# One two-bank PSUM tile for both pairs of heads, and one operation for both, in the attention's products

## The chip, the cores and the metric

The kernel runs on one core of one Trainium2 chip. The metric is the device time of the whole kernel in microseconds (us), as the median of several runs.

## The reference

Two layers follow each other. The first is attention by the delta rule, with 4 batches, 8 heads, 768 steps and a head width of 48:

```python
k_n = k / (norm(k) + 1e-6)
for t in range(S):
    y[:, :, t] = einsum('bhd,bhde->bhe', q[:, :, t], state)
    v_old = einsum('bhde,bhd->bhe', state, kt)
    state = state + bt * einsum('bhd,bhe->bhde', kt, vt - v_old)
```

The second is a rational feed-forward layer on the 3072 rows of 384 that the attention gives (`d_ff` is 2048):

```python
h = x @ w_in
P = a[0] + a[1]*h + a[2]*h**2 + a[3]*h**3
Q = 1 + |b[0]|*|h| + |b[1]|*h**2
out = (P / (Q + 1e-6)) @ w_out
```

## The kernel before

The 768 steps are cut into 12 chunks of 64. A chunk of all four batches is worked at once: 128 partitions are two batches by 64 steps, and the other factor of two of the batches is the **pair** `p` (`PAIRS`, two of them), each with 8 heads. So a product of the attention has 16 small results of 48 or 64 columns, 8 for each pair. `mm3` (L401) makes them: for each pair 24 matmuls (8 heads, 3 passes of float16 halves), first pair 0, then pair 1. `bank` (L418) gives each pair a PSUM tile of its own, one bank of 512 float32 columns. ACT and DVE then take the result out with an operation for each pair, so twice for each product, each on 8*48 = 384 or 8*64 = 512 columns.

A chunk goes through these products: `pg` (keys by keys, taken out by ACT at L528), `pm` (keys by queries, DVE, L667), `pe` (blocks off the diagonal, `split16` at L614), `pk` (the state's part of the residual, DVE, L687), `pu` (the solve), `pd` (the state's update, DVE, L719) and `py` (the outputs, ACT, L734). The solve is a chain: `solve_start` writes `pu`, and three times `solve_step` (L698) reads `pu`, makes two float16 halves `z` of it (ACT writes the upper half at L229, DVE the rest at L233), and adds the product of `z` to `pu`. `solved` reads `pu` once more (ACT L227, DVE L231), `state_next` multiplies that and adds it to the state `S16`, and the next chunk's `state_split`, `residual` and solve start from `S16`. So the chunks' solves form one chain through the kernel. `tokens` (L739) scales the outputs of a chunk and transposes them into `xT`, with `px` in PSUM and `split16` at L762.

The feed-forward layer takes a chunk's `xT` in 8 **units** `n` (96 in all): `hidden` multiplies (`ph`, L818), `numerator` and `quotient` compute the fraction (L835 to L865, each operation on 512 columns; `mu`, `mw`, `mr` and `mg` are their tiles), and `accumulate` multiplies into `po` (L880). Unit 8c is the first of chunk c and can't start before `xT` of chunk c and the scalars `msc` (L802) are there.

PSUM has 8 banks: `ps_f` two tiles of a bank (`pg`, `pm`, `pe`, small totals, and `px` from chunk 3 on), `ps_c` two (`pk`, `pu`, `pd`, `py`, and `px` of the first chunks), `ps_h` two, `ps_o` two. The order of the instructions on each engine comes from a scheduler that places them by priorities and by its own estimates (L1054); the attention's steps of chunks c+1 to c+4 are issued among the units of chunk c (`attention`, L977), and those of the solve with a raised priority. Each engine then runs its instructions strictly in the order so found.

Of the kernel before, what the change touches and what calls it, by code (L numbers as in the profile page):

```python
# [36 lines left out]
def kernel(  # L37
# [29 lines left out]
    TG = NPAIR * P  # L67
# [13 lines left out]
    sb = ctx.enter_context(tc.tile_pool(name="sb", bufs=2))  # L81
    dpool = ctx.enter_context(tc.tile_pool(name="dpool", bufs=2, space=DRAM))
    dfix = ctx.enter_context(tc.tile_pool(name="dfix", bufs=1, space=DRAM))
    ps_f = ctx.enter_context(tc.tile_pool(name="ps_f", bufs=2, space=PSUM))
    ps_c = ctx.enter_context(tc.tile_pool(name="ps_c", bufs=2, space=PSUM))
    ps_h = ctx.enter_context(tc.tile_pool(name="ps_h", bufs=2, space=PSUM))
    ps_o = ctx.enter_context(tc.tile_pool(name="ps_o", bufs=1, space=PSUM))

# [148 lines left out]
    def parts(t):  # L237
        return t[:, 0], t[:, 1]
# [5 lines left out]
        nc.gpsimd.tensor_scalar(x, x, scale, 0.0, op0=ALU.mult, op1=ALU.add)  # L244

    def total(src, n, nm, pool=ps_f, tag="a"):
        pf = pool.tile([P, n], F32, tag=tag, name="pf" + nm)
        nc.tensor.matmul(pf, ones, src, start=True, stop=True)
        return pf

# [166 lines left out]

    def bank(pool, nm, w):  # L418

        made = []  # L420
        for p in PAIRS:
            t = pool.tile([P, 512], F32, tag="a", name=f"{nm}_{p}")
            made.append(t[:, : H * w].rearrange("p (h w) -> p h w", w=w))
        return made

    def of(t, p):

        return t[:, p * H : (p + 1) * H]

    def of_parts(t, p):  # L430
        return of(t[:, 0], p), of(t[:, 1], p)
# [29 lines left out]
    def transposed(x, src, nm, soon):  # L461


        split16(
            [x[:, i, :, :, :D].rearrange("p h b d -> p b h d") for i in range(2)],
            src.rearrange("p (b h) d -> p b h d", b=2),
            eng=nc.gpsimd,
            hi=nc.gpsimd,
        )
        xd = dpool.tile([2, NH, P, HG, 2, DP], F16, tag="xd" + nm[0], name=f"xd{nm}", bufs=4 if nm[0] == "k" else 2)  # L470
        nc.sync.dma_start(
            out=xd.rearrange("i n r a b d -> r (i n) (a b d)"),
            in_=x.rearrange("r i (n a) b d -> r (i n) (a b d)", n=NH),
        )
        t = sb.tile([P, 2, NH, NPAIR, C, HG], F16, tag="tt", name="t" + nm)
        if soon:
            for i in range(2):
                pt = ps_f.tile([P, H, P], F16, tag="a", name=f"pt{nm}_{i}")
                for h in range(H):
                    nc.tensor.transpose(pt[:, h], x[:, i, h].rearrange("p b d -> p (b d)"), ident16)  # L480
                for n in range(NH):
                    nc.scalar.copy(
                        t[:, i, n].rearrange("x p t a -> x a (p t)"), pt[:, n * HG : (n + 1) * HG]
                    )
            return t, xd
        nc.sync.dma_start(
            out=t.rearrange("x i n p t a -> x (i n p t a)"),
            in_=xd.rearrange("i n r a b d -> (i n r a) (b d)"),
            transpose=True,
        )  # L490
        return t, xd
# [29 lines left out]
    def key_products(c):  # L521
        d = info[c]
        gd = d["gd"] = dpool.tile([P, BS], F32, tag="gd", name=f"gd_{c}")
        pg = bank(ps_f, f"pg_{c}", C)
        mm3(pg, d["kbd"], d.pop("tk"))
        g = sb.tile([P, HP, C], F32, tag="g", name=f"g_{c}", bufs=1)
        for p in PAIRS:
            nc.scalar.mul(of(g, p), pg[p], -1.0)  # L528
        for b in range(2):
            nc.sync.dma_start(out=as_rows(gd, b), in_=g[b * C : (b + 1) * C])  # L530
        gl = sb.tile([P, HP, C - 16, 2], F16, tag="gl", name=f"gl_{c}", bufs=1)
        split16([gl[..., i] for i in range(2)], g[:, :, : C - 16], eng=nc.gpsimd, hi=nc.gpsimd)
        d["gl"] = gl
# [71 lines left out]
    def off_blocks(c):  # L605

        d = info[c]
        gbd, wc = d.pop("gbd"), d.pop("wc")
        pe = bank(ps_f, f"pe_{c}", C - 16)
        mm3(pe, gbd, wc[:, :, 16:])  # L610
        d["wbd"] = to_diagonal("w", wc)
        et = sb.tile([P, 2, HP, C - 16], F16, tag="u0", name=f"et_{c}", bufs=1)
        for p in PAIRS:
            split16(of_parts(et, p), pe[p], 1.0 / 256.0)  # L614
        ebd = d["ebd"] = diag["e"][0]
        for b in range(2):
# [43 lines left out]
    def query_products(c):  # L660

        d = info[c]
        pm = bank(ps_f, f"pm_{c}", C)
        mm3(pm, d["kbd"], d["tq"])
        m32 = sb.tile([P, HP, C], F32, tag="g", name=f"m32_{c}", bufs=1)
        for p in PAIRS:
            nc.vector.tensor_mul(of(m32, p), pm[p], mask.unsqueeze(1).broadcast_to([P, H, C]))  # L667
        mm = d["mm"] = sb.tile([P, 2, NG, C, HG], F16, tag="mm", name=f"mm_{c}", bufs=1)
        split16([alternating(mm[:, i]) for i in range(2)], grouped(m32), eng=nc.gpsimd)

# [9 lines left out]
    def residual(c):  # L680
        d = info[c]
        rf = d.pop("vs")
        if c > 0:
            pk = bank(ps_c, f"pk_{c}", D)
            mm3(pk, d["kbd"], d["sh"])
            for p in PAIRS:
                nc.vector.scalar_tensor_tensor(  # L687
                    out=of(rf, p), in0=of(rf, p), scalar=d["sv"], in1=pk[p], op0=ALU.mult, op1=ALU.subtract
                )
        d["rr"] = sb.tile([P, 2, HP, D], F16, tag="z", name=f"rr_{c}", bufs=2)  # L690
        split16(parts(d["rr"]), rf, eng=nc.gpsimd)

# [5 lines left out]
    def solve_step(c, it):  # L698

        d = info[c]  # L700
        z = sb.tile([P, 2, HP, D], F16, tag="z", name=f"z_{c}_{it}", bufs=2)
        for p in PAIRS:
            split16(of_parts(z, p), d["pu"][p], zmask[:, it : it + 1])
        mm3(d["pu"], d["ebd"], z, start=False)

    def solved(c):
        d = info[c]
        d["z"] = sb.tile([P, 2, HP, D], F16, tag="z", name=f"z_{c}", bufs=2)
        pu = d.pop("pu")
        for p in PAIRS:  # L710
            split16(of_parts(d["z"], p), pu[p])

    def state_next(c):
        d = info[c]
        pd = bank(ps_c, f"pd_{c}", D)
        mm3(pd, d["knbd"], d["z"])
        if c > 0:
            for p in PAIRS:
                nc.vector.scalar_tensor_tensor(  # L719
                    out=of(S16, p), in0=pd[p], scalar=d["isv"], in1=of(S16, p), op0=ALU.mult, op1=ALU.add  # L720
                )
        else:
            for p in PAIRS:
                nc.scalar.activation(of(S16, p), pd[p], AF.Copy, scale=d["isv"])

    def outputs(c):
        d = info.pop(c)
        py = bank(ps_c, f"py_{c}", D)
        if c > 0:
            mm3(py, d["qbd"], d["sh"], stop=False)  # L730
        mm3(py, d["mbd"], d["z"], start=c == 0)
        y = ys[c] = sb.tile([P, NPAIR, DM], F32, tag="ob", name=f"y_{c}", bufs=1)
        for p in PAIRS:
# [5 lines left out]
    def tokens(c):  # L739
# [318 lines left out]
```

## Time and profile before

| what | value |
|---|---|
| runs shown | 890.34, 892.65, 892.75 us; median 892.65 us |
| profiled execution, its own time | 895.27 us |
| its span | 893.4 us |
| busy: DVE | 800.4 us (90%) |
| busy: PE | 675.1 us (76%) |
| busy: ACT | 579.7 us (65%) |
| busy: POOL | 468.4 us (52%) |

The engines run side by side, so the busy times overlap. The first of the 96 units starts its DVE work at 151.26 us; before that the weights are converted and chunk 0 goes through the attention. The view by line gives for each group of instructions the busy time, the mean duration of one, and the idle time ahead of them. The view by time gives the starts, from which one sees how long an instruction really keeps its engine: the next one often starts before the last has ended.

### The profile page before, as it was taken

The page shows a single profiled execution, that of the slowest core. Times are in us where ns is not written, and L with a number is a line of the kernel's source. Part 1 is how long each engine was busy: PE and PEld are TensorE (multiplying, and loading weights), DVE is VectorE, ACT ScalarE, POOL GpSimd, SP SyncE. Part 2 cuts the span into 40 slices and gives each one's busy share as a digit, 9 for nine tenths or more (in the row PEclk, how much of TensorE's full clock was granted, in tenths as well). Part 3 has the DMA queues.
Part 4 walks back from the last instruction along what each step waited for, and adds up shares of the span by engine and source line. Part 5 has one row for each costly group of instructions (what it writes and reads, how often), then busy time and mean ns, then how long its engine had stood idle before and what let it go on. Part 6 is the DMA issues. An engine that isn't in the chain of part 4 may idle for free.

```text
span 893.4 us, 23555 instructions
## 1 busy us (share of the span) xinstructions
PE 675.1 (76%) x9264; PEld 540.8 (61%) x9264; DVE 800.4 (90%) x1666; ACT 579.7 (65%) x1122; POOL 468.4 (52%) x430
## 2 busy tenths in 40 slices
PE   0231454878597697988859989969989799899885
PEld 0221444766485585766648757758767677777563
DVE  5999898898888779879998799999999999898996
ACT  4776766647665483857657657667669476878574
POOL 6664754626446245466654574754745645353622
PEclk9999976978998897999988999989999899999998
DMA  8969978578858867879377469487485553200000
GB/s 234 231 165 196 207 173 158 95 144 143 160 115 147 172 136 137 140 144 186 57 164 123 95 132 167 79 181 139 84 191 94 112 108 58 67 1 19 1 19 18
DMA packets 420110, 111.49 MB, mean 125 GB/s; under 512 B 361376, under 2 KB 416672, under 8 KB 420000
## 3 DMA queue, kind: packets, MB, share of 16 engines
q1 hardware_dynamic: 417824, 108.83, 61.8%
q8 instruction: 72, 1.18, 0.6%
q10 hardware_dynamic: 2176, 1.17, 0.4%
q14 instruction: 38, 0.31, 0.1%
HBM read 40.47 MB, written 26.23 MB: 75 GB/s over the span
## 4 chain that ended last, share of the span: by engine, by line
DVE 33%; PE 22%; DMA 15%; SPq 11%; issue 8%; ACT 8%; POOL 3%; ACTq 0%; DVEq 0%; POOLq 0%
PE ph L818 7%; PE po L880 5%; SPq L441 4%; DVE mw L860 3%; DMA tq<-xdq 3%; PE pg L409 3%; DVE mu L838 2%; DVE mu L864 2%; DVE w_out L333 2%; DVE mw L840 2%; PE pm L409 2%; DVE mg L859 2%; PE pu L409 2%; DVE mu L842 2%; DMA wc<-img 2%
## 5 line engine op out<-in xcount | busy, mean ns | idle before, releaser
L818 PE MATMUL ph<-xT,w_in 128*128 128x256 f16 x1728 | 225.9, 286 | 30.3 <-DVE mu L842 29.5
L880 PE MATMUL po<-w_out,mg 128*128 128x384 f16 x1152 | 223.3, 340 | 28.8 <-POOL mg L865 27.0
L818 PEld LDWEIGHTS <-w_in 128*128 128x128 f16 x1728 | 174.1, 103 | 67.7 <-issue 18.1
L865 POOL TENSOR_TENSOR mg<-mu,mr 128x512 f16<-128x512 f32 x96 | 133.2, 1391 | 92.6 <-DVE mu L864 53.7
L880 PEld LDWEIGHTS <-mg 128*128 128x128 f16 x1152 | 110.5, 102 | 101.9 <-POOL mg L865 33.7
L835 ACT ACTIVATE mu<-ph,coef,msc 128x512 f32<-128x512 f32 x96 | 74.4, 775 | 60.7 <-DVE msc L802 25.0
L409 PEld LDWEIGHTS <-kbd 128*128 128x128 f16 x1680 | 93.6, 119 | 33.0 <-issue 28.2
L860 DVE SCALAR_TENSOR_TENSOR mw<-mw,msc,mg 128x512 f32<-128x512 f32 x96 | 88.0, 918 | 0.4
L838 DVE TENSOR_TENSOR mu<-ph,mu 128x512 f32<-128x512 f32 x96 | 65.5, 682 | 23.8 <-ACT mr L837 22.9
L841 ACT ACTIVATE mw<-mw 128x512 f32<-128x512 f32 x96 | 60.4, 630 | 35.5 <-DVE mw L840 35.1
L862 POOL TENSOR_TENSOR mu<-mu,mw 128x512 f32<-128x512 f32 x36 | 51.1, 1421 | 50.2 <-DVE mw L860 20.3
L840 DVE SCALAR_TENSOR_TENSOR mw<-mr,msc,ph 128x512 f32<-128x512 f32 x96 | 70.7, 737 | 0.0
L842 DVE SCALAR_TENSOR_TENSOR mu<-mu,msc,ph 128x512 f32<-128x512 f32 x96 | 70.5, 735 | 0.0
L853 ACT ACTIVATE mr<-mw,msc 128x512 f32<-128x512 f32 x96 | 69.2, 721 | 1.1
L409 PE MATMUL pu<-z,ebd 128*128 128x48 f16 x1728 | 56.1, 187 | 16.1 <-DVE z L233 12.3
L409 PEld LDWEIGHTS <-ebd 128*128 128x128 f16 x1728 | 54.5, 99 | 21.1 <-issue 19.0
L837 ACT ACTIVATE mr<-ph,msc 128x512 f32<-128x512 f32 x96 | 65.6, 684 | 0.0
L231 POOL TENSOR_TENSOR mm<-m,mm 128x1024 f16<-128x1024 f32 x12 | 31.6, 2632 | 64.0 <-ACT mm L227 56.2
L859 DVE SCALAR_TENSOR_TENSOR mg<-mu,msc,mr 128x512 f16<-128x512 f32 x60 | 60.7, 1012 | 2.5 <-ACT mr L854 2.5
L409 PEld LDWEIGHTS <-wbd 128*128 128x128 f16 x1152 | 37.1, 102 | 40.3 <-issue 26.2
L854 ACT ACTIVATE mr<-mr 128x512 f32<-128x512 f32 x96 | 60.4, 630 | 1.4
L846 POOL TENSOR_SCALAR mu<-mu,msc 128x512 f32<-128x512 f32 x36 | 28.9, 802 | 55.2 <-DVE mu L842 52.1
(201 smaller groups left out, 1435.7 us busy)
## 6 DMA issues: line engine op xcount, KB each, us to landing
wsi<-in_moe_w_in_dram SPq DMA_DIRECT2D x24, 256.0 KB, 4.9
xdk<-kn SPq DMA_DIRECT2D x12, 512.0 KB, 4.3
kbd<-tk SPq DMA_DIRECT2D x24, 256.0 KB, 4.3
gd<-g SPq DMA_DIRECT2D x24, 256.0 KB, 3.4
xdq<-kn SPq DMA_DIRECT2D x12, 512.0 KB, 3.5
wso<-in_moe_w_out_dram SPq DMA_DIRECT2D x32, 192.0 KB, 4.4
mbd<-mm SPq DMA_DIRECT2D x24, 256.0 KB, 4.9
wc<-img SPq DMA_DIRECT2D x24, 256.0 KB, 4.9
```

The costliest lines, as they stand in the source:

```text
L409: nc.tensor.matmul(dst[p][:, h], head(bd, lp, p * H + h), head(rt, rp, p * H + h), start=start and n == 0 and h == 0, stop=stop and n == l ...
L818: nc.tensor.matmul(ph[:, i], w_in[:, f2, wp, cc, i * P : (i + 1) * P], x[:, xp, cc], start=k == 0, stop=k == 3 * NCC - 1,)
L835: nc.scalar.activation(u, ph, AF.Identity, scale=A3, bias=a2)
L837: nc.scalar.activation(z, ph, AF.Abs, scale=B1)
L838: nc.vector.tensor_mul(u, ph, u)
L840: nc.vector.scalar_tensor_tensor(out=w, in0=z, scalar=B0, in1=ph, op0=ALU.add, op1=ALU.mult)
L842: nc.vector.scalar_tensor_tensor(out=u, in0=u, scalar=A1, in1=ph, op0=ALU.add, op1=ALU.mult)
L853: nc.scalar.activation(r, w, AF.Ln, bias=Q0)
L859: nc.vector.scalar_tensor_tensor(out=g[:, 0], in0=u, scalar=A0, in1=r, op0=ALU.add, op1=ALU.mult)
L860: nc.vector.scalar_tensor_tensor(out=w, in0=w, scalar=Q0, in1=g[:, 0], op0=ALU.add, op1=ALU.mult)
L865: nc.gpsimd.tensor_mul(g[:, 1], u, r)
L880: nc.tensor.matmul(po[p], g[:, gp, i, p * P : (p + 1) * P], w_out[:, f2, wp, i], start=f2 == lo and i == 0 and k == 0, stop=f2 == hi - 1 a ...
```

## The change

`bank` makes one tile of two banks, and gives a view for each pair and one of both. The pools `ps_f` and `ps_c` have one such tile each in the place of two of one bank. All matmuls stay, pair 0 first, each into a bank of its pair. Each operation that takes a product out covers both pairs: 768 columns in the place of twice 384, 1024 in the place of twice 512. In `tokens` the total, its copy to all partitions and the transposes share one tile, and the split covers both pairs. For `ps_f` every other user (`total`, the transposes of the first chunk) takes the whole tile of two banks.

```diff
+    ps_f = ctx.enter_context(tc.tile_pool(name="ps_f", bufs=1, space=PSUM))
+    ps_c = ctx.enter_context(tc.tile_pool(name="ps_c", bufs=1, space=PSUM))
...
     def total(src, n, nm, pool=ps_f, tag="a"):
-        pf = pool.tile([P, n], F32, tag=tag, name="pf" + nm)
+        pf = pool.tile([P, NPAIR * 512 if pool is ps_f else n], F32, tag=tag, name="pf" + nm)[:, :n]
...
     def bank(pool, nm, w):
-        made = []
-        for p in PAIRS:
-            t = pool.tile([P, 512], F32, tag="a", name=f"{nm}_{p}")
-            made.append(t[:, : H * w].rearrange("p (h w) -> p h w", w=w))
-        return made
+        t = pool.tile([P, NPAIR, 512], F32, tag="a", name=nm)[:, :, : H * w].rearrange("x p (h w) -> x p h w", w=w)
+        return t[:, 0], t[:, 1], t
+
+    def by_pair(t):
+        return t.rearrange("x (p h) d -> x p h d", p=NPAIR)
+
+    def parts_by_pair(t):
+        return by_pair(t[:, 0]), by_pair(t[:, 1])
...
         g = sb.tile([P, HP, C], F32, tag="g", name=f"g_{c}", bufs=1)
-        for p in PAIRS:
-            nc.scalar.mul(of(g, p), pg[p], -1.0)
+        nc.scalar.mul(by_pair(g), pg[2], -1.0)
...
-        for p in PAIRS:
-            split16(of_parts(et, p), pe[p], 1.0 / 256.0)
+        split16(parts_by_pair(et), pe[2], 1.0 / 256.0)
...
-        for p in PAIRS:
-            nc.vector.tensor_mul(of(m32, p), pm[p], mask.unsqueeze(1).broadcast_to([P, H, C]))
+        nc.vector.tensor_mul(
+            m32, pm[2].rearrange("x p h t -> x (p h) t"), mask.unsqueeze(1).broadcast_to([P, HP, C])
+        )
...
-            for p in PAIRS:
-                nc.vector.scalar_tensor_tensor(
-                    out=of(rf, p), in0=of(rf, p), scalar=d["sv"], in1=pk[p], op0=ALU.mult, op1=ALU.subtract
-                )
+            nc.vector.scalar_tensor_tensor(
+                out=by_pair(rf), in0=by_pair(rf), scalar=d["sv"], in1=pk[2], op0=ALU.mult, op1=ALU.subtract
+            )
...
         z = sb.tile([P, 2, HP, D], F16, tag="z", name=f"z_{c}_{it}", bufs=2)
-        for p in PAIRS:
-            split16(of_parts(z, p), d["pu"][p], zmask[:, it : it + 1])
+        split16(parts_by_pair(z), d["pu"][2], zmask[:, it : it + 1])
         mm3(d["pu"], d["ebd"], z, start=False)
...
-        for p in PAIRS:
-            split16(of_parts(d["z"], p), pu[p])
+        split16(parts_by_pair(d["z"]), pu[2])
...
-            for p in PAIRS:
-                nc.vector.scalar_tensor_tensor(
-                    out=of(S16, p), in0=pd[p], scalar=d["isv"], in1=of(S16, p), op0=ALU.mult, op1=ALU.add
-                )
+            nc.vector.scalar_tensor_tensor(
+                out=by_pair(S16), in0=pd[2], scalar=d["isv"], in1=by_pair(S16), op0=ALU.mult, op1=ALU.add
+            )
...
-        for p in PAIRS:
-            nc.scalar.activation(y[:, p].rearrange("p (h d) -> p h d", h=H), py[p], AF.Copy, scale=d["iy"])
+        nc.scalar.activation(y.rearrange("x p (h d) -> x p h d", h=H), py[2], AF.Copy, scale=d["iy"])
...
+        px = pool.tile([P, NPAIR * 512], F32, tag="a", name=f"px_{c}")
+        pf, pb = px[:1, NCC * TG : NCC * TG + P], px[:, NCC * TG + P : NCC * TG + P + 1]
...
+        px = px[:, : NCC * TG].rearrange("x (c t) -> x c t", t=TG)
         for p in PAIRS:
-            px = pool.tile([P, 512], F32, tag="a", name=f"px_{c}_{p}")[:, : NCC * P].rearrange("p (c t) -> p c t", t=P)
             for cc in range(NCC):
-                nc.tensor.transpose(px[:, cc], yt[:, p, cc * P : (cc + 1) * P], identf)
-            split16([x[:, i, :, p * P : (p + 1) * P] for i in range(2)], px, sx)
+                nc.tensor.transpose(px[:, cc, p * P : (p + 1) * P], yt[:, p, cc * P : (cc + 1) * P], identf)
+        split16(parts(x), px, sx)
```

The scheduler finds another order for the whole kernel. Two places on DVE show it. In the names the first number is the chunk or the unit, and `z_2_1` is `z` of the second solve step of chunk 2; the changed file's lines lie a few lower or higher.

DVE, from the second to the third solve step of chunk 2, before:

```order
L233 SCALAR_TENSOR_TENSOR z_2_1_3498<-pu_2_0_3231,zmask_85,z_2_1_3498 128x384
L233 SCALAR_TENSOR_TENSOR z_2_1_3498<-pu_2_1_3232,zmask_85,z_2_1_3498 128x384
L842 SCALAR_TENSOR_TENSOR mu9_3609<-mu9_3609,msc_1_3174,ph_9_3590 128x512
L859 SCALAR_TENSOR_TENSOR mg8_3620<-mu8_3482,msc_1_3174,mr8_3484 128x512
L576 TENSOR_REDUCE ab_3_2568<-pr_3_2567 128x64
L838 TENSOR_TENSOR mu10_3867<-ph_10_3848,mu10_3867 128x512
L840 SCALAR_TENSOR_TENSOR mw10_3872<-mr10_3869,msc_1_3174,ph_10_3848 128x512
L860 SCALAR_TENSOR_TENSOR mw8_3487<-mw8_3487,msc_1_3174,mg8_3620 128x512
L578 TENSOR_TENSOR pr_3_2567<-ab_3_2568,wt0_111 128x512
L233 SCALAR_TENSOR_TENSOR z_2_2_3625<-pu_2_0_3231,zmask_85,z_2_2_3625 128x384
L842 SCALAR_TENSOR_TENSOR mu10_3867<-mu10_3867,msc_1_3174,ph_10_3848 128x512
L233 SCALAR_TENSOR_TENSOR z_2_2_3625<-pu_2_1_3232,zmask_85,z_2_2_3625 128x384
```

The same place now:

```order
L234 SCALAR_TENSOR_TENSOR z_2_1_3426<-pu_2_3164,zmask_85,z_2_1_3426 128x768
L851 SCALAR_TENSOR_TENSOR mg10_4009<-mu10_3786,msc_1_3107,mr10_3788 128x512
L852 SCALAR_TENSOR_TENSOR mw10_3791<-mw10_3791,msc_1_3107,mg10_4009 128x512
L830 TENSOR_TENSOR mu12_4124<-ph_12_4105,mu12_4124 128x512
L832 SCALAR_TENSOR_TENSOR mw12_4129<-mr12_4126,msc_1_3107,ph_12_4105 128x512
L856 SCALAR_TENSOR_TENSOR mu10_3786<-mu10_3786,msc_1_3107,mw10_3791 128x512
L834 SCALAR_TENSOR_TENSOR mu12_4124<-mu12_4124,msc_1_3107,ph_12_4105 128x512
L502 TENSOR_REDUCE nrm_5_3732<-sq_5_3733 128x16
L851 SCALAR_TENSOR_TENSOR mg11_4135<-mu11_3998,msc_1_3107,mr11_4000 128x512
L234 SCALAR_TENSOR_TENSOR z_2_2_3551<-pu_2_3164,zmask_85,z_2_2_3551 128x768
```

Each step is one row of 768 columns that needs both pairs' matmuls and ACT's whole operation; between the two steps of pair 0 stood 7 rows of other work, and now 8 stand between the steps.

DVE ahead of unit 24, the first of chunk 3, before (the two rows of `S16` are the end of chunk 4's solve):

```order
L719 SCALAR_TENSOR_TENSOR S16_133<-pd_4_0_6185,sc_4_3560,S16_133 128x384
L719 SCALAR_TENSOR_TENSOR S16_133<-pd_4_1_6186,sc_4_3560,S16_133 128x384
L860 SCALAR_TENSOR_TENSOR mw21_5440<-mw21_5440,msc_2_4324,mg21_5523 128x512
L778 TENSOR_SCALAR kp_3_0_5452<-kp_3_0_5452,coef_99 128x1 x3
L838 TENSOR_TENSOR mu23_5618<-ph_23_5599,mu23_5618 128x512
L840 SCALAR_TENSOR_TENSOR mw23_5623<-mr23_5620,msc_2_4324,ph_23_5599 128x512
L233 SCALAR_TENSOR_TENSOR xT_3_5377<-px_3_0_5392,sf_3_5379,xT_3_5377 128x3x128
L233 SCALAR_TENSOR_TENSOR xT_3_5377<-px_3_1_5398,sf_3_5379,xT_3_5377 128x3x128
L259 TENSOR_SCALAR kp_3_0_5452<-kp_3_0_5452 128x1
L778 TENSOR_SCALAR kp_3_0_5452<-kp_3_0_5452 128x1
L857 TENSOR_TENSOR mg22_5629<-mu22_5511,mr22_5513 128x512
L842 SCALAR_TENSOR_TENSOR mu23_5618<-mu23_5618,msc_2_4324,ph_23_5599 128x512
```

The same place now:

```order
L234 SCALAR_TENSOR_TENSOR xT_3_5261<-px_3_5265,sf_3_5263,xT_3_5261 128x768
L778 RECIPROCAL kp_3_0_5331<-kp_3_0_5331 128x2
L232 TENSOR_TENSOR z_4_6045<-pu_4_5407,z_4_6045 128x768
L260 TENSOR_SCALAR kp_3_0_5331<-kp_3_0_5331,coef_99 128x1
L770 TENSOR_SCALAR kp_3_0_5331<-kp_3_0_5331 128x1
L782 TENSOR_SCALAR kp_3_0_5331<-kp_3_0_5331,coef_99,top_138 128x1
L783 TENSOR_SCALAR kp_3_0_5331<-kp_3_0_5331 128x1
L253 TENSOR_SCALAR kp_3_0_5331<-kp_3_0_5331 128x1
L787 RECIPROCAL kp_3_0_5331<-kp_3_0_5331 128x1
L258 TENSOR_SCALAR kp_3_0_5331<-kp_3_0_5331 128x1
L258 TENSOR_SCALAR sf_3_5263<-sf_3_5263,kp_3_0_5331 128x1
L713 SCALAR_TENSOR_TENSOR S16_133<-pd_4_6048,sc_4_3486,S16_133 128x768
```

Before, chunk 4's solve and the state's update were done while units 21 to 23 still had rows left, and `mu24` came 28 rows after the last row printed. Now units up to 23 are done before the first row printed, `z_4` and `S16` stand in the scalar work ahead of unit 24, and `mu24` comes 5 rows after the last row printed.

## Rows read from the trace of the kernel before

**Rows 1.** Busy time and share of the span, by engine, from the page.

```profile
PE 675.1 (76%) x9264; PEld 540.8 (61%) x9264; DVE 800.4 (90%) x1666; ACT 579.7 (65%) x1122; POOL 468.4 (52%) x430
```

**Rows 2.** By stretches of 50 us: engines' busy us (count), clock, DMA share, GB/s.

```profile
280.00:330.00 50.00, 41.66 (x643) 34.65 (x641) 40.06 (x93) 28.81 (x55) 19.41 (x18) 0.87 0.75 150
...
580.00:630.00 50.00, 42.49 (x640) 35.46 (x639) 48.18 (x98) 35.43 (x62) 27.54 (x22) 0.93 0.76 150
```

**Rows 3.** By line and shape, DVE: count | busy us, mean ns | idle before.

```profile
L233 DVE SCALAR_TENSOR_TENSOR z<-pu,zmask,z 128x384 f16<-128x384 f32 x72 | 43.0, 607 | 7.8 <-ACT z L229 7.8
...
L667 DVE TENSOR_TENSOR m<-pm,mask 128x512 f32<-128x512 f32 x24 | 16.4, 684 | 6.2 <-PE pm L409 5.8
...
L233 DVE SCALAR_TENSOR_TENSOR xT<-px,sf,xT 128x384 f16<-128x384 f32 x24 | 14.0, 605 | 0.0
...
L687 DVE SCALAR_TENSOR_TENSOR v<-v,sc,pk 128x384 f32<-128x384 f32 x22 | 13.1, 607 | 0.5 <-PE pk L409 0.2
...
L231 DVE TENSOR_TENSOR z<-pu,z 128x384 f16<-128x384 f32 x24 | 13.0, 548 | 6.5 <-ACT z L227 6.3
L233 DVE SCALAR_TENSOR_TENSOR et<-pe,et 128x384 f16<-128x384 f32 x24 | 12.8, 544 | 1.5 <-ACT et L229 1.5
...
L719 DVE SCALAR_TENSOR_TENSOR S<-pd,sc,S 128x384 f32<-128x384 f32 x20 | 11.8, 603 | 0.2
```

**Rows 4.** In order of time, DVE: start us, duration us, instruction, count.

```profile
614.72 1.12 DVE L233 SCALAR_TENSOR_TENSOR z<-pu,zmask,z 128x384 f16<-128x384 f32 x2
615.77 0.73 DVE L859 SCALAR_TENSOR_TENSOR mg<-mu,msc,mr 128x512 f16<-128x512 f32 x1
...
619.19 0.68 DVE L838 TENSOR_TENSOR mu<-ph,mu 128x512 f32<-128x512 f32 x1
619.79 0.74 DVE L840 SCALAR_TENSOR_TENSOR mw<-mr,msc,ph 128x512 f32<-128x512 f32 x1
620.45 0.15 DVE L252 TENSOR_SCALAR sf<-lgx 128x1 uint32<-128x1 uint32 x1
...
627.85 0.55 DVE L231 TENSOR_TENSOR z<-pu,z 128x384 f16<-128x384 f32 x1
628.32 0.74 DVE L842 SCALAR_TENSOR_TENSOR mu<-mu,msc,ph 128x512 f32<-128x512 f32 x1
```

**Rows 5.** One solve step in order of time, PE, then ACT, then DVE.

```profile
300.84 1.37 PE L409 MATMUL pu<-rr,wbd 128*128 128x48 f16 x48
...
301.64 1.19 ACT L229 ACTIVATE z<-pu,zmask 128x384 f16<-128x384 f32 x2 [7.11 <-PE pu L409]
302.73 2.50 ACT L227 CAST mm<-m 128x1024 f16<-128x1024 f32 x1
...
302.26 0.62 DVE L233 SCALAR_TENSOR_TENSOR z<-pu,zmask,z 128x384 f16<-128x384 f32 x1 [1.18 <-ACT z L229]
```

**Rows 6.** What DVE waited for: us in total, times, longest us.

```profile
DVE mu L838 <- ACT mr L837: 22.9, 21, 4.3
DVE z L233 <- ACT z L229: 7.8, 8, 3.1
...
DVE z L231 <- ACT z L227: 6.3, 5, 1.6
...
DVE m L667 <- PE pm L409: 5.8, 4, 2.5
```

**Rows 7.** Stretches of 25 us that end where units 16, 24, 32 and 48 start.

```profile
297.89:322.89 25.00, 21.10 (x388) 17.70 (x386) 17.50 (x39) 13.70 (x26) 8.44 (x6) 0.90 0.77 151
...
368.42:393.42 25.00, 22.22 (x342) 18.32 (x340) 20.91 (x52) 14.95 (x34) 15.42 (x16) 1.00 0.71 131
...
436.16:461.16 25.00, 20.93 (x372) 17.97 (x371) 23.14 (x58) 11.88 (x25) 15.74 (x12) 0.98 0.57 111
...
564.79:589.79 25.00, 20.81 (x369) 17.74 (x368) 24.83 (x62) 13.73 (x30) 18.28 (x17) 1.00 0.45 89
```

More of the change, by code (lines that the diff above doesn't have):

```diff
@@ L83 @@
     dfix = ctx.enter_context(tc.tile_pool(name="dfix", bufs=1, space=DRAM))
-    ps_f = ctx.enter_context(tc.tile_pool(name="ps_f", bufs=2, space=PSUM))
-    ps_c = ctx.enter_context(tc.tile_pool(name="ps_c", bufs=2, space=PSUM))
+    ps_f = ctx.enter_context(tc.tile_pool(name="ps_f", bufs=1, space=PSUM))
+    ps_c = ctx.enter_context(tc.tile_pool(name="ps_c", bufs=1, space=PSUM))
     ps_h = ctx.enter_context(tc.tile_pool(name="ps_h", bufs=2, space=PSUM))
@@ L418, in bank @@
     def bank(pool, nm, w):
-        made = []
-        for p in PAIRS:
-            t = pool.tile([P, 512], F32, tag="a", name=f"{nm}_{p}")
-            made.append(t[:, : H * w].rearrange("p (h w) -> p h w", w=w))
-        return made
[L426 to L431, printed above, removed]
+        t = pool.tile([P, NPAIR, 512], F32, tag="a", name=nm)[:, :, : H * w].rearrange("x p (h w) -> x p h w", w=w)
[4 more added lines that the diff above has]
+        return by_pair(t[:, 0]), by_pair(t[:, 1])
     def to_diagonal(nm, t, c=0):
@@ L476, in transposed @@
         if soon:
+            pts = ps_f.tile([P, 2, H, P], F16, tag="a", name=f"pt{nm}")
             for i in range(2):
-                pt = ps_f.tile([P, H, P], F16, tag="a", name=f"pt{nm}_{i}")
+                pt = pts[:, i]
                 for h in range(H):
@@ L717, in state_next @@
         if c > 0:
-            for p in PAIRS:
-                nc.vector.scalar_tensor_tensor(
-                    out=of(S16, p), in0=pd[p], scalar=d["isv"], in1=of(S16, p), op0=ALU.mult, op1=ALU.add
-                )
-        else:
-            for p in PAIRS:
-                nc.scalar.activation(of(S16, p), pd[p], AF.Copy, scale=d["isv"])
+            nc.vector.scalar_tensor_tensor(
+                out=by_pair(S16), in0=pd[2], scalar=d["isv"], in1=by_pair(S16), op0=ALU.mult, op1=ALU.add
+            )
+        else:
+            nc.scalar.activation(by_pair(S16), pd[2], AF.Copy, scale=d["isv"])
     def outputs(c):
@@ L732, in outputs @@
         y = ys[c] = sb.tile([P, NPAIR, DM], F32, tag="ob", name=f"y_{c}", bufs=1)
-        for p in PAIRS:
-            nc.scalar.activation(y[:, p].rearrange("p (h d) -> p h d", h=H), py[p], AF.Copy, scale=d["iy"])
+        nc.scalar.activation(y.rearrange("x p (h d) -> x p h d", h=H), py[2], AF.Copy, scale=d["iy"])
     toks = {}
@@ L749, in tokens @@
         sum_squares(fs, yt.rearrange("p a e -> p (a e)"), x[:, 0].rearrange("p c t -> p (c t)"))
-        pf = pool.tile([1, P], F32, tag="a", name=f"pfx{c}")
+        px = pool.tile([P, NPAIR * 512], F32, tag="a", name=f"px_{c}")
+        pf, pb = px[:1, NCC * TG : NCC * TG + P], px[:, NCC * TG + P : NCC * TG + P + 1]
         nc.tensor.transpose(pf, fs, identf)
         nc.vector.tensor_reduce(xm[:1], pf, axis=AX.X, op=ALU.max)
-        pb = pool.tile([P, 1], F32, tag="a", name=f"pb{c}")
         nc.tensor.matmul(pb, ones[:1], xm[:1], start=True, stop=True)
```

## The prediction

> **What bounds the kernel now.** I read the page's busy times first. DVE is the fullest engine, 800.4 of 893.4 us, and ACT has a third of its time free [rows 1]. Then the stretches of 50 us, because an average can hide two regimes. It does: from 580 to 630 us DVE is busy 48.18 of 50 us, from 280 to 330 us only 40.06 [rows 2]. Late in the kernel, DVE work is time almost one for one. Early, something else holds the chain of work, and DVE waits for it. The stretches that end where a chunk's first unit starts show where: in the 25 us ahead of unit 16 DVE is busy 17.50 us, so idle 7.50; ahead of unit 24 it is idle 4.09, ahead of unit 32 1.86 and ahead of unit 48 0.17 [rows 7]. Ahead of unit 16 the solve of chunk 3 runs while the units of chunk 1 have run out, so that DVE has nothing to put between the solve's steps. Last, the waits of DVE: 22.9 us behind ACT's L837, which a unit's start needs, and 7.8, 6.3 and 5.8 us behind the attention's products (8, 5 and 4 times) [rows 6].
>
> **What the change removes.** Half of the instructions that take products out. On DVE these are, by half the counts in [rows 3]: 36 for `z` in the three solve steps, 12 for `xT`, 11 for `v`, 10 for `S`, together 69 of the form with a scalar from memory; and 12 for the last `z`, 12 for `et`, 12 for `m`, together 36 that are quicker. On ACT 97 go: 36 and 12 for `z`, 12 each for `g`, `et`, `y` and `xT`, one for `S`. The columns stay as many, and so do the matmuls.
>
> What one is worth is not its duration, since the next one starts before it has ended. So I go by start to start where DVE had no gap [rows 4]. Two `z` of 384 columns keep it from 614.72 to 615.77, 1.05 us. One operation of this form with 512 columns keeps it from 619.79 to 620.45, 0.66 us. The slope is (0.66 - 0.525) / 128 = 1.05 ns a column, so 768 columns should take 0.66 + 256 x 1.05 ns = 0.93 us: 0.12 us less than two halves. The quicker form takes 0.47 us for 384 columns (627.85 to 628.32) and 0.60 for 512 (619.19 to 619.79), a slope of 1.02 ns, hence 0.86 us for 768 in the place of 0.94, and 1.12 for 1024 in the place of 1.20: 0.08 us less. `et` has the mean of this form (544 ns beside 548) and goes with it [rows 3]. The sum is 69 x 0.12 + 36 x 0.08 = 8.3 + 2.9 = **11.2 us** of DVE.
>
> Both ends of this term: no row of the trace reads two banks with one instruction. If such a read fell apart into two, the saving would be 0. If the starts didn't overlap, the whole fixed part of the durations would go, which is 607 less 384 columns at 1.05 ns, or 204 ns, for the first kind and 548 - 392 = 156 ns for the second, in all 19.7 us. I take 11.2, since it comes from rows of the same shapes in a full stretch. A loss here would need a two-bank read that is slower than its two halves one after the other, and no row hints at one.
>
> [...]
>
> On ACT two `z` halves end 1.19 us after the first began [rows 5]; whatever one operation saves there lies on an engine that is free for a third of the time, so I count nothing. What hides it is DVE's work; if DVE's cover were gone, it would be a part of the 22.9 us of waits behind L837.
>
> **What the change adds.** Pairs no longer overtake each other. Before, ACT could take pair 0 while PE still worked on pair 1: the 48 matmuls of `pu` run from 300.84 for 1.37 us and ACT starts at 301.64, and DVE starts on pair 0 at 302.26, while ACT finishes pair 1 [rows 5]. Now ACT waits for all 48, and DVE for ACT's whole operation. Where nothing else is queued, a step gets longer by the half of the matmuls (0.69 us) and by up to half of ACT's two operations (0.6 us): 0 to 1.3 us a step, the lower end where other rows stand between. The order shows such rows at the second and third step of chunk 2, 8 now where 7 stood. So most steps stay covered, and I don't put 1.3 us on each of the 17 waits of [rows 6].
>
> The steps that are not covered are those ahead of a chunk's first unit, after the last row of the unit before. By the order, four steps of chunk 3's solve (`z_3_1`, `z_3_2`, `z_3`, `S16`) stood there ahead of unit 16, and cost the 7.50 us of [rows 7], 1.9 us each. Now two stand there (`z_3_0`, `z_3_1`), but ahead of unit 24, where none stood, there are three (`z_4_2`, `z_4`, `S16`). Five in the place of four: one more at 1.9 us, and all five longer by something between 0 and 1.3 us, of which I take 0.5 since a good part of such a gap is filled by the scalar work that stands there. That gives back 1.9 + 5 x 0.5 = **4.4 us**, with ends at 0 (the steps are covered) and 1.9 + 5 x 1.3 = 8.4.
>
> PSUM: `ps_f` and `ps_c` now pass from one product to the next as a whole. A matmul of the next product waits for the whole copy-out of the last one, where it could begin on pair 0's bank before. On PE the row behind it waits too, mostly `ph` and `po` of the units. PE is free for a quarter of the time [rows 1], and only `pfq`, `pk` and `py` follow closely on another product, so I count nothing; a bound from above is half an ACT copy, 0.6 us, for some 30 of them, which is 18 us if each of them were on the path.
>
> **The sum.** 893.4 - 11.2 + 4.4 = 886.6 us of span, 888.5 for the profiled execution's own time of 895.27. That execution is 2.6 us above the median of 892.65 us, so the forecast for the median is 892.65 - 6.8 = 885.85, say 885.8 us.
>
> **Rivals.**
> Starved boundaries (slower). The solve's steps pile up ahead of units 24 and 32, as they did ahead of unit 16. For it: the order has three of them ahead of unit 24 now, and between `z_4` and `S16` only eight small scalar rows, while 48 matmuls and their wait lie between; `S16`, `sh_6` and `et_6` stand ahead of unit 32. Against it: ahead of unit 32 an `S16` and `sh_6` stood before, and cost only 1.86 us. Price: ahead of unit 24 the 7.50 us of unit 16 and 5 steps longer by 1.1, which is 13.0 in the place of 4.09; ahead of unit 32 7.50 in the place of 1.86; and 0.3 us on each of 17 waits. Together 8.9 + 5.6 + 5.1 = 19.6 us against the saving of 11.2: 892.65 + 8.4 = **901 us**. It decides from the point where the new idle time of DVE exceeds 11.2 us.
> [...]
>
> The two-bank read saves nothing (same). The change does what it says in the count of instructions, but an operation on two banks costs as much as its halves. For it: no row shows one. Against it: the slope between 384 and 512 columns is that of plain columns [rows 4]. Time: 892.65 + 0 to 2 = **893 us**.
>
> ACT is freed and DVE waits less (faster than forecast). Of the 22.9 us behind L837 [rows 6] a third goes, since 97 instructions less stand in ACT's queue, and nothing is given back: 892.65 - 11.2 - 7.6 = **874 us**. Against it: most of these waits stand at a chunk's first unit, where ACT waits itself for `xT` and PE.
>
> **How the numbers follow.** A measurement of this kernel can tell about 0.3%, 2.7 us, from no change. The forecast (881 to 890 us) gets 0.42, the greater gain (below 881) 0.18, no saving (890 to 895.3) 0.16, starved boundaries (above) 0.24. So faster 0.60, same 0.16, slower 0.24. The likeliest case's own range is 881 to 890. The range for 8 in 10 reaches from 871, where the upper end of the saving is nearly all kept, to 902, just past the price of the starved boundaries.
>
> **What would show it.** Right: DVE's count falls by 105 and its busy time by 10 to 20 us; `z` of 768 columns takes about 0.93 us from start to start; the idle time of DVE grows by less than 6 us; ahead of unit 16 it is smaller and ahead of unit 24 larger than in [rows 7]. Wrong: DVE's busy time falls and its idle time grows by more than 11 us (starved boundaries; the waits behind ACT's `z` grow, or those of PE on the copies out of PSUM); `z` of 768 columns keeps DVE for 1.05 us (no saving); or DVE waits less behind L837 (greater gain). What I can't foresee is the order's other shifts, since the scheduler places every row anew.

## The result and the profile after

The changed kernel takes 882.98 us (median of 4 runs, 881.47 to 884.28) against 892.7 us (890.34 to 895.12) for the kernel before on the same chip: a ratio of 0.989, 95% interval 0.987 to 0.991, so 9.7 us less. The forecast was 885.8 us, 6.8 less. The profiled execution took 883.2 us, its span is 881.5 us. Busy times and counts of the kernel after, which answer to [rows 1]:

```profile
PE 664.4 (75%) x9264; PEld 534.4 (61%) x9264; DVE 784.8 (89%) x1561; ACT 568.5 (64%) x1025; POOL 474.3 (54%) x430
```

The span is 11.9 us shorter. DVE is busy 15.6 us less with 105 instructions less, and idle 881.5 - 784.8 = 96.7 us where it was idle 93.0. By line and shape, DVE, for comparison with [rows 3]:

```profile
L234 DVE SCALAR_TENSOR_TENSOR z<-pu,zmask,z 128x768 f16<-128x768 f32 x36 | 36.3, 1007 | 6.3 <-ACT z L230 6.2
...
L232 DVE TENSOR_TENSOR z<-pu,z 128x768 f16<-128x768 f32 x12 | 11.4, 946 | 0.0
...
L713 DVE SCALAR_TENSOR_TENSOR S<-pd,sc,S 128x768 f32<-128x768 f32 x10 | 10.1, 1010 | 8.8 <-PE pd L410 8.8
```

And in order of time (start, duration), for comparison with [rows 4]:

```profile
612.64 1.00 DVE L234 SCALAR_TENSOR_TENSOR z<-pu,zmask,z 128x768 f16<-128x768 f32 x1
613.57 0.14 DVE L253 TENSOR_SCALAR sf<-lgx 128x1 uint32<-128x1 uint32 x1
...
634.03 0.94 DVE L232 TENSOR_TENSOR z<-pu,z 128x768 f16<-128x768 f32 x1
634.90 0.19 DVE L794 TENSOR_TENSOR msc<-tab,sf 128x48 f32<-128x48 f32 x1
```

A `z` of 768 columns keeps DVE from 612.64 to 613.57, 0.93 us, and the last `z` 0.87 us: in these rows one instruction on two banks costs its columns and one fixed part (0.93 and 0.86 us by the slopes of [rows 4]). Added up over all DVE instructions that [rows 3] lists as taking a product out, from each start to the next start or to the end if that comes first, DVE is held for 110.2 us before (210 instructions) and 98.8 us after (105): **11.4 us less**. The other 4.2 us by which its busy time fell lie in instructions that the change doesn't touch; the last section shows where such a difference can come from.

The 25 us that end where units 16, 24, 32 and 48 start, for comparison with [rows 7] (columns: stretch, its length, busy us and count of PE, PEld, DVE, ACT, POOL, then clock, DMA share, GB/s):

```profile
281.29:306.29 25.00, 17.00 (x264) 13.98 (x263) 18.56 (x47) 10.67 (x20) 10.85 (x6) 0.86 0.78 163
358.49:383.49 25.00, 21.50 (x362) 18.21 (x362) 14.98 (x36) 13.33 (x23) 9.81 (x9) 0.93 0.86 169
428.66:453.66 25.00, 23.17 (x398) 19.30 (x395) 20.79 (x50) 14.67 (x28) 15.35 (x16) 0.93 0.45 80
549.07:574.07 25.00, 23.58 (x356) 19.36 (x356) 23.99 (x56) 17.92 (x36) 16.64 (x17) 0.99 0.58 107
```

DVE is idle 6.44, 10.02, 4.21 and 1.01 us there, where it was 7.50, 4.09, 1.86 and 0.17. The longest of the waits in the 10.02 us ahead of unit 24 (the second row above) are these (start, duration; in brackets the idle time ahead and what ended it):

```profile
361.61 1.22 DVE L663 TENSOR_TENSOR m<-pm,mask 128x1024 f32<-128x1024 f32 x1 [2.73 <-PE pm L410]
...
369.12 1.02 DVE L234 SCALAR_TENSOR_TENSOR z<-pu,zmask,z 128x768 f16<-128x768 f32 x1 [1.77 <-ACT z L230]
...
376.99 0.15 DVE L253 TENSOR_SCALAR kp<-kp 128x1 uint32<-128x1 uint32 x1 [2.40 <-ACT kp L785]
...
379.14 1.02 DVE L713 SCALAR_TENSOR_TENSOR S<-pd,sc,S 128x768 f32<-128x768 f32 x1 [1.30 <-PE pd L410]
```

So the solve's steps make 3.1 us of it, `m` 2.7 and a scalar row 2.4. Over the whole kernel, DVE's longest waits (total, times, longest), for [rows 6]:

```profile
DVE mu L830 <- ACT mr L829: 18.7, 18, 2.3
DVE S L713 <- PE pd L410: 8.8, 4, 2.9
DVE m L663 <- PE pm L410: 8.4, 5, 2.7
DVE z L234 <- ACT z L230: 6.2, 7, 2.6
```

`S` and `m`, which need both pairs' matmuls now, wait 8.8 - 0.2 and 8.4 - 5.8 us longer; `mu` waits 4.2 us less and the last `z` 6.3 less.

### The profile page after: what moved, and what is told of

Same layout as the page of the kernel before. It is cut to its first block, busy times and chain, and to the rows that moved or that the text cites. A ratio compares the mean times of both kernels' runs of the same rounds, so it can differ in the third digit from the quotient of the medians.

```text
span 881.5 us, 23343 instructions
## 1 busy us (share of the span) xinstructions
PE 664.4 (75%) x9264; PEld 534.4 (61%) x9264; DVE 784.8 (89%) x1561; ACT 568.5 (64%) x1025; POOL 474.3 (54%) x430
## 4 chain that ended last, share of the span: by engine, by line
DVE 29%; PE 18%; DMA 18%; SPq 14%; issue 9%; ACT 7%; POOL 3%; POOLq 0%; ACTq 0%; DVEq 0%
PE ph L810 6%; PE po L872 4%; SPq L616 4%; DVE mw L852 3%; PE pg L410 3%; DMA kbd<-tk 3%; SPq L119 3%; SPq L439 3%; DVE mu L834 2%; DVE w_out L334 2%; DVE mu L830 2%; DMA xdq<-kn 2%; DVE mw L832 2%; DVE mg L851 2%; DVE mu L856 2%
## 5 line engine op out<-in xcount | busy, mean ns | idle before, releaser
L872 PE MATMUL po<-w_out,mg 128*128 128x384 f16 x1152 | 216.6, 333 | 22.6 <-POOL mg L857 20.7
L857 POOL TENSOR_TENSOR mg<-mu,mr 128x512 f16<-128x512 f32 x96 | 135.5, 1412 | 96.5 <-DVE mu L856 70.6
L852 DVE SCALAR_TENSOR_TENSOR mw<-mw,msc,mg 128x512 f32<-128x512 f32 x96 | 93.4, 973 | 0.4
L830 DVE TENSOR_TENSOR mu<-ph,mu 128x512 f32<-128x512 f32 x96 | 65.5, 683 | 20.6 <-ACT mr L829 18.7
L832 DVE SCALAR_TENSOR_TENSOR mw<-mr,msc,ph 128x512 f32<-128x512 f32 x96 | 70.6, 735 | 0.0
L834 DVE SCALAR_TENSOR_TENSOR mu<-mu,msc,ph 128x512 f32<-128x512 f32 x96 | 70.3, 733 | 0.0
L851 DVE SCALAR_TENSOR_TENSOR mg<-mu,msc,mr 128x512 f16<-128x512 f32 x60 | 55.7, 928 | 2.1 <-ACT mr L846 2.1
L856 DVE SCALAR_TENSOR_TENSOR mu<-mu,msc,mw 128x512 f32<-128x512 f32 x60 | 52.3, 871 | 0.2
L410 PE MATMUL pg<-tk,kbd 128*128 128x64 f16 x576 | 38.5, 241 | 18.1 <-DMA kbd<-tk 10.6
```

Of the source, the lines that this page charges most:

```text
L410: nc.tensor.matmul(dst[p][:, h], head(bd, lp, p * H + h), head(rt, rp, p * H + h), start=start and n == 0 and h == 0, stop=stop and n == l ...
L830: nc.vector.tensor_mul(u, ph, u)
L832: nc.vector.scalar_tensor_tensor(out=w, in0=z, scalar=B0, in1=ph, op0=ALU.add, op1=ALU.mult)
L834: nc.vector.scalar_tensor_tensor(out=u, in0=u, scalar=A1, in1=ph, op0=ALU.add, op1=ALU.mult)
L851: nc.vector.scalar_tensor_tensor(out=g[:, 0], in0=u, scalar=A0, in1=r, op0=ALU.add, op1=ALU.mult)
L852: nc.vector.scalar_tensor_tensor(out=w, in0=w, scalar=Q0, in1=g[:, 0], op0=ALU.add, op1=ALU.mult)
```

## The experiments

The change does four things at once: merged operations on DVE, merged ones on ACT, tiles of two banks, and a new order for all engines, since the scheduler places everything anew. The first four kernels leave the order to the scheduler. The other eight are given an order: a list of instruction numbers for each engine, made from another kernel's order, in which two halves stand where the merged operation stood and the other way round. Ratios are to the kernel before measured beside the run, with 95% intervals: it took 891.83 us beside the first four, 896.15 beside before_oa, after_ot, t_split and dve_oa, and 895.16 beside the others. Expectations in microseconds were worked out from 892.65 us, so where the two differ the ratio decides. No kernel was given its own order as a control, so that giving an order costs nothing by itself is not shown.

### Parts of the change, with the order that the scheduler finds

All four have the tiles of two banks. `MA` and `MD` name the operations that are merged on ACT and on DVE.

```diff
+    def halves(merged, *aps):
+        if merged:
+            return [aps]
+        return [tuple(a[:, p] for a in aps) for p in PAIRS]
...
-            nc.vector.scalar_tensor_tensor(
-                out=by_pair(rf), in0=by_pair(rf), scalar=d["sv"], in1=pk[2], op0=ALU.mult, op1=ALU.subtract
-            )
+            for o, i in halves('v' in MD, by_pair(rf), pk[2]):
+                nc.vector.scalar_tensor_tensor(
+                    out=o, in0=o, scalar=d["sv"], in1=i, op0=ALU.mult, op1=ALU.subtract
+                )
```

**tile_only**: nothing merged (`MA` and `MD` empty).

> The two-bank tile and the pools of the change, but every operation on a product still once for each pair, on ACT and on DVE. Theory A (the time comes from the fixed part of the DVE instructions that the change takes away): DVE's busy time is back near 800 us and the time is 890 to 898 us. Rival B (the two-bank tile or the pools bring it): near 883 us. Rival C (it is only that the scheduler found a better order): anywhere from 880 to 905 us, with no tie to the count of DVE instructions.

924.21 us, 1.036 (1.034 to 1.039), above all three ranges. **dve_merged**: everything on DVE merged, ACT by pairs.

```diff
+    MA = set()
+    MD = {'g','et','m','v','z','zf','S','y','xT'}
```

> As the change, but ACT keeps an operation for each pair; DVE has one for both. Theory A: DVE's operations lose their 11 us as in the change, the time is 881 to 887 us. Rival D (it is ACT's 97 instructions, through DVE's waits on ACT): 888 to 893 us.

878.18 us, 0.985 (0.982 to 0.987), below both ranges. **act_merged**: the two sets exchanged.

> As the change, but DVE keeps an operation for each pair; ACT has one for both. Theory A: DVE keeps its 800 us, and each solve step waits for ACT's whole operation, so 891 to 899 us. Rival D: near 883 us.

891.06 us, 1.000 (0.998 to 1.002), at the low end of theory A's range. **solve_merged**: `z`, the last `z`, `v` and `S` merged on both engines; `g`, `et`, `m`, `y` and `xT` by pairs.

```diff
+    MA = {'z','zf','S','v'}
+    MD = {'z','zf','S','v'}
```

> Both engines merged for the solve and the state alone (z in the solve's steps, the last z, v and S); g, et, m, y and xT stay once for each pair, on the two-bank tile. Theory A: 8.3 of the 11.4 us of DVE are saved, and the longer steps stay, so 884 to 890 us. Rival C: no relation to these 8.3 us.

901.63 us, 1.011 (1.009 to 1.014), far above theory A's range, although these operations hold 8.3 of the 11.4 us that DVE saves.

With the two-bank tile alone the kernel is 3.6% slower, and with one engine's operations merged it is even (act_merged) or faster (dve_merged). But these four have four different orders, so none of the ratios belongs to one cause. What each operation costs can only be compared in one order.

### The same operations in another kernel's order

```diff
+    order = json.loads(zlib.decompress(base64.b64decode(ORDER_TABLE)))
+    made = {i.name: i for i in nc.cur_bb.bb.instructions}
+    info = mybir.DependencyInfo(mybir.DependencyClass.NoSync, mybir.DependencyReason.DATA)
+    for names in order.values():
+        for a, b in zip(names, names[1:]):
+            tc.add_manual_dep(made[f"I-{b}"], f"I-{a}", info, reason="order")
```

**before_oa**: the kernel before, with its tiles of one bank and all its 1666 DVE instructions, in the order of the kernel after (this diff, and `_force(tc, nc)` at the end).

> The kernel before, with its tiles of one bank and an operation for each pair, but on every engine in exactly the order of the changed kernel (each pair of operations stands where the one for both stood). Theory A (the fixed part of 105 DVE instructions is what is gained): DVE's busy time is back near 796 to 800 us, and the time is 888 to 895 us, a little less than 11 us above the changed kernel because pair 0 may again run ahead of pair 1. Rival C (the scheduler's new order is what is gained): 881 to 885 us.

887.49 us, 0.989 (0.987 to 0.992): the whole gain of the change, with no operation merged. In microseconds it lies between the two ranges; scaled to the 896.15 us measured beside it, they are 891.5 to 898.5 for theory A and 884.5 to 888.5 for rival C, which holds it. Its page:

```profile
PE 661.2 (75%) x9264; PEld 531.1 (60%) x9264; DVE 790.7 (89%) x1666; ACT 579.4 (65%) x1122; POOL 474.7 (54%) x430
```

Its products still hold DVE for 110.3 us, as before. So the 11.4 us aren't needed for the gain: a kernel without them, in the same order, is as fast.

**after_ot**: the reverse, the kernel after in the order of tile_only.

> All operations merged as in the changed kernel, but on every engine in the order that the scheduler found for the two-bank tile with split operations (924 us). Theory A: the merged operations are worth their 11 us in this order as well, so 909 to 915 us. Rival C: 920 us or more, since the order alone sets the time.

926.73 us, 1.034 (1.031 to 1.037). The same instructions as in the kernel after, 1561 on DVE, take 4.5% longer in another order. In this order merging everything brings nothing measurable (1.036 to 1.034). The kernel before wasn't run in it, so how much of the 1.036 is the order's and how much the tiles' stays open.

**after_ob**: the kernel after in the order of before; a merged operation stands where pair 1's stood, and pair 0's matmuls move down to pair 1's.

> All operations merged as in the changed kernel, in the order of the kernel before on every engine; a merged operation stands where pair 1's stood, and so do the product's matmuls of pair 0. Theory A: a ratio near 0.99. Theory E (the scheduler's new order is the gain, and in the old order the coarser waits cost what the merging saves): 0.997 or more.

919.99 us, 1.026 (1.023 to 1.029). Its page, and two of its waits:

```profile
PE 685.3 (75%) x9264; PEld 547.4 (60%) x9264; DVE 779.9 (85%) x1561; ACT 568.4 (62%) x1025; POOL 467.6 (51%) x430
```

```profile
DVE mu L830 <- ACT mr L829: 28.6, 26, 3.7
DVE z L234 <- ACT z L230: 16.5, 11, 5.3
```

DVE's busy time falls as in the kernel after, to 779.9 us, but it idles 139.6 us. These two waits grew by 5.7 and 8.7 us, 14.4 of the 46.6 us by which the idle time is above that of the kernel before. In this order, made for halves, the whole-tile waits were not covered. A part of this may be the experiment's own, since the matmuls that move down can delay what follows them on PE; how large that part is was not measured.

Then the order of dve_merged, the fastest so far, with the kernel before (**before_od**) and with the kernel after (**after_od**).

> The kernel before (tiles of one bank, an operation for each pair), in exactly the order that the scheduler found with DVE merged and ACT not (a ratio of 0.985 there). Theory E: 0.983 to 0.990, the order's gain without any merging. Theory A: 0.996 or more.

> The changed kernel in exactly the order that the scheduler found with DVE merged and ACT not. It may beat the changed kernel. Theory E: as that one, 0.982 to 0.987. Theory A says the same, since DVE's work is the same in both; if ACT's merging were a gain of its own, below 0.982.

881.3 us, 0.985 (0.982 to 0.989) and 884.5 us, 0.987 (0.985 to 0.990). Split or merged makes no measurable difference here, and dve_merged itself stands at 0.985. The page of before_od:

```profile
PE 664.8 (76%) x9264; PEld 532.1 (61%) x9264; DVE 796.0 (91%) x1666; ACT 577.4 (66%) x1122; POOL 479.4 (55%) x430
```

With a span of 878.4 us, DVE is idle 82.4 us, 10.6 less than in the kernel before.

### The parts of the change in the order of after

**dve_oa** (`MD` full, `MA` empty), **act_oa** (`MA` full, `MD` empty) and **t_split** (both empty) have the tiles of two banks and the order of the kernel after.

> The changed kernel's tiles and order, DVE with one operation for both pairs, ACT with one for each pair. Theory A: ACT's merged operations are worth little, so 881 to 886 us. Rival D (ACT's 97 instructions count): 887 us or more.

> The changed kernel's tiles and exactly its order, ACT with one operation for both pairs, DVE with one for each. Its waits are as coarse as the changed kernel's, so this isolates DVE's merging. Theory A (DVE's 11 us are gained in full): a ratio to the kernel before near 1.001. Theory E (of the 11 us little reaches the end, since the order sets the time): 0.989 to 0.995.

> The changed kernel's two-bank tiles and exactly its order on every engine, but each operation on a product split into its two halves, one behind the other. Theory A: 11 us more of DVE, and waits no finer than the changed kernel's, so 892 to 898 us. Rival C: 881 to 886 us, and the 924 us of the two-bank tile with split operations in the scheduler's own order were the order's.

| in the order of after | tiles of | DVE | ACT | us | ratio, 95% |
|---|---|---|---|---|---|
| before_oa | one bank | halves | halves | 887.49 | 0.989 (0.987 to 0.992) |
| t_split | two banks | halves | halves | 948.62 | 1.059 (1.056 to 1.061) |
| act_oa | two banks | halves | merged | 891.76 | 0.996 (0.993 to 0.998) |
| dve_oa | two banks | merged | halves | 888.13 | 0.992 (0.989 to 0.995) |
| the kernel after | two banks | merged | merged | 882.98 | 0.989 (0.987 to 0.991) |

t_split lies above both ranges of its expectation. dve_oa is in rival D's range in microseconds, but scaled to 896.15 us theory A's range is 884.5 to 889.5, which holds it. act_oa lies between theory E's 0.995 and theory A's 1.001, and nearer to E.

Here the order is one, so rows may be subtracted. Merging on DVE is worth 0.9955 - 0.989 = 0.65%, some 5.8 us of the 11.4 by which DVE's work shrinks; by the intervals this is good to about 3 us, as is the next difference. Merging on ACT is worth 0.992 - 0.989, with intervals that overlap, so not shown to be other than nothing. Going from one-bank halves to two-bank tiles with ACT merged costs 0.9955 - 0.9891, some 5.7 us: that is the price of the coarser waits, of tiles and pools together, less whatever ACT's merging gives. Gain and price cancel, and what is left of the change in this order is nothing that can be measured: 0.989 both times.

Of this price, in one profiled execution each, 3.3 us lie behind the start of unit 24: that stretch takes 503.1 us in act_oa, with DVE idle 45.2, and 499.8 in before_oa, with DVE idle 37.6 (its row is below).

```profile
386.67:889.80 503.13, 432.14 (x5810) 340.84 (x5809) 457.92 (x876) 332.81 (x558) 265.32 (x212) 0.96 0.52 99
```

Units 8 to 23 take 1.6 us more in act_oa, and what is ahead of them 1.8 us less.

With the tile alone (before_oa to t_split, 0.989 to 1.059) the price is 7% in one order: halves must not be left on a common tile. One solve step of it in order of time, first ACT, then DVE (start, duration; in brackets what ended the idle time ahead):

```profile
319.36 0.57 ACT L230 ACTIVATE z<-pu,zmask 128x384 f16<-128x384 f32 x1
320.62 0.58 ACT L230 ACTIVATE z<-pu,zmask 128x384 f16<-128x384 f32 x1 [0.69 <-DVE z L234]
```

```profile
319.97 0.61 DVE L234 SCALAR_TENSOR_TENSOR z<-pu,zmask,z 128x384 f16<-128x384 f32 x1
321.23 0.62 DVE L234 SCALAR_TENSOR_TENSOR z<-pu,zmask,z 128x384 f16<-128x384 f32 x1 [0.65 <-ACT z L230]
```

ACT's half for pair 1 needs nothing from DVE, yet it starts only when DVE is through with pair 0 (319.97 + 0.61 = 320.58). In the 48 pairs of `z`, ACT's second half started ahead of the end of DVE's first in 39 cases before, in 48 of before_oa, in 0 of t_split. The two kernels with this order and these halves, before_oa and t_split, differ in the tiles and their pools alone. So the wait that the program sets goes by the tile, as far as these rows show, and the tile now holds both pairs: two engines that read different banks take turns in all 48 pairs of `z`. ACT's longest waits for DVE's halves in t_split, over the kernel (total, times, longest):

```profile
ACT z L230 <- DVE z L234: 78.8, 36, 5.5
ACT et L230 <- DVE et L234: 36.4, 12, 4.4
```

These are not among ACT's waits in the kernel before. In before_oa the two halves lie in different banks as well, each on a tile of its own, and there ACT and DVE run side by side (48 of 48): so the wait in t_split is wider than the bank. Halves on one tile without that wait were not tried. The wait also gives solve_merged's 1.011 a likely reason, since its `et` and `xT` are halves on a common tile, but its order is another too.

### Where an order gains

Nothing but the order differs between the kernel before and before_oa. From the start of unit 8 to that of unit 24 (columns as above):

```profile
234.30:393.40 159.10, 128.59 (x1944) 105.63 (x1944) 133.72 (x265) 95.34 (x176) 76.48 (x63) 0.90 0.76 149
393.40:893.40 500.00, 431.53 (x5662) 340.01 (x5662) 461.31 (x865) 337.44 (x610) 261.12 (x207) 0.94 0.50 96
```

and the same stretches of before_oa:

```profile
237.20:386.90 149.70, 122.85 (x1891) 100.64 (x1889) 123.04 (x249) 94.08 (x170) 69.84 (x56) 0.91 0.74 139
386.90:886.70 499.80, 427.44 (x5811) 338.98 (x5809) 462.21 (x876) 339.47 (x614) 267.93 (x212) 0.96 0.52 99
```

Units 8 to 23 take 149.7 us in the place of 159.1, and all that follows 499.8 in the place of 500.0. In the kernel after the two are 150.0 and 498.0. The gain is made by unit 24, in the early part, where chunks 2 to 4 are solved. Unit 8 starts 2.9 us later (237.2), so the span of the profiled execution is 2.9 - 9.4 - 0.2 = -6.7 us different. DVE does 16 instructions fewer in units 8 to 23, and those that come later don't make the rest longer. In the whole kernel before_oa's DVE is busy 9.7 us less and idle 3.0 us more with the same instructions; the last section shows where such busy time can come from. By its count, the time by which DVE's instructions in units 8 to 23 exceed their group's quick ones falls from 18.8 to 11.1 us, most of the 10.7 us by which DVE is busy less there; its idle time doesn't fall (25.4 and 26.7 us). In before_od units 8 to 23 take 143.2 us, and there the idle time falls, to 11.7, while that excess is 24.2. So an order can gain in two ways, and which rows of it do so was not settled, nor why the scheduler finds a better order for the merged operations.

## Why the prediction was right, and where it was not

- **DVE's fixed part**: 11.2 us foreseen, 11.4 measured. The start-to-start reading of [rows 4] held, with 0.93 us for 768 columns as worked out. The end of 0 (a two-bank read that falls apart) and that of 19.7 (the durations) are both out.
- **The give-back**: 4.4 us foreseen, DVE's idle time grew by 3.7. Its places were right in sign: 1.1 us less ahead of unit 16, 5.9 us more ahead of unit 24. But only 3.1 of the 10.02 us ahead of unit 24 are the solve's steps, the rest is mostly `m` and a scalar row; ahead of unit 32 2.4 us came that I hadn't counted, and behind ACT's `mr` DVE waited 4.2 us less. The 3.7 is a net of terms that I didn't have, so that it is near 4.4 is luck.
- **ACT counted nothing**: not contradicted. dve_oa and the kernel after, which differ in ACT's 97 instructions, are 0.3% apart with overlapping intervals.
- **The pools that pass as a whole, counted nothing**: not settled. In the fixed order the coarser waits of pools and tiles together cost 5.7 us, give or take 3. The sum had 4.4 us for the tiles, so what the pools cost by themselves isn't shown; the bound of 18 us holds.
- **The sum was right as a number, and wrong as a cause.** It took 11.2 us off the span as if the order stayed. before_oa reaches 0.989 without a saved microsecond; in the order of after the merging on DVE brings 5.8 us and the coarser waits take 5.7. So one step that failed is to count DVE's 11.2 us as span one for one: about half of it arrived. The other is the last sentence of "What would show it": the order's other shifts were named as something that can't be foreseen and given no term. Taken in the new order, they were the whole net change, 9.7 us; in the old order the same edits cost 2.6%. That the order gave 9.7 us where the terms summed to 6.8 is luck.
- **The rivals.** Starved boundaries: 10.02 us of idle time ahead of unit 24 and 4.21 ahead of unit 32 are near its 13.0 and below its 7.50, but DVE's idle time grew by 3.7 us in all and not by its 19.6. In the old order (after_ob) it is just what happens: DVE saves its time, idles 139.6 us, and the kernel is 2.6% slower. The greater gain: the waits behind `mr` fell from 22.9 to 18.7 us, 4.2 of its 7.6, but it had nothing given back, and DVE's idle time grew. The one that saves nothing fell with the first point.
- What stays open: why the order came out better, and which of its rows do it. And dve_merged's 0.985 (0.982 to 0.987) touches the interval of the kernel after, so it isn't shown to be the better one.

## What to carry to other kernels

Where a scheduler places everything anew, a change of operations is two changes: run the old operations in the new order before the gain is put down to the operations. Merging operations over two PSUM banks took the fixed part off here (11.4 us for 105 instructions, 0.11 us each), but the wait got as wide as the tile, and in the one order where both were measured it cost what the merging brought (5.7 and 5.8 us). If a tile holds what two engines take in halves (1.059 in that order), merge the halves on one of them at least (0.996 and 0.992), or give each half its own tile (0.989).

## What was not expected of the hardware

The same DVE instruction doesn't always take the same time: L852 below takes from 0.65 to 2.89 us. By line and shape in the kernel after:

```profile
L852 DVE SCALAR_TENSOR_TENSOR mw<-mw,msc,mg 128x512 f32<-128x512 f32 x96 | 93.4, 973 | 0.4
L832 DVE SCALAR_TENSOR_TENSOR mw<-mr,msc,ph 128x512 f32<-128x512 f32 x96 | 70.6, 735 | 0.0
L834 DVE SCALAR_TENSOR_TENSOR mu<-mu,msc,ph 128x512 f32<-128x512 f32 x96 | 70.3, 733 | 0.0
```

The three have one operation and one shape. L832 and L834 read `ph` from PSUM, and in all their 192 executions none is longer than 0.75 us. L852 reads both its tensors from SBUF; most take 0.74 us, but 25 of 96 are longer by over 0.1, up to 2.89 us. A POOL operation overlaps 116 of the 192, and none is longer for it; it overlaps 51 of the 96, among them all 25 long ones. Two of `mg`, also from SBUF alone, in the kernel before, then POOL at the same time:

```profile
601.80 1.97 DVE L859 SCALAR_TENSOR_TENSOR mg<-mu,msc,mr 128x512 f16<-128x512 f32 x1
...
604.95 0.74 DVE L859 SCALAR_TENSOR_TENSOR mg<-mu,msc,mr 128x512 f16<-128x512 f32 x1
```

```profile
601.58 1.64 POOL L231 TENSOR_TENSOR rr<-v,rr 128x768 f16<-128x768 f32 x1 [0.76 <-ACT rr L227]
```

In the kernel before, 196 DVE instructions are longer by over 0.1 us than the quick tenth of their group (the same operation, tiles and shape), 129.5 us in all or 14% of the span, and 190 of them have a POOL operation beside them. It is 118.8 us in before_oa, 10.7 less with the same instructions, beside 9.7 us by which its busy time fell; so the order alone changed how much of it there is. For the three lines above, the executions that read PSUM are never long (0 of 192), and those that read SBUF alone are long in 25 of 96, each time beside POOL. Why these alone are long is not shown. No run took POOL's work away, so the cause is read from the traces and not tested.
